# Grouped-query attention on one core: the P·V product of two groups as full-array matmuls of 256 columns in place of column-tiled ones

## The chip, the core and the metric

The kernel runs on one core of a Trainium2 chip. The metric is the device time of one execution in microseconds; the kernel before takes 348.19 us (median of three runs, 348.05 to 348.26). The profiled execution has a span of 346.9 us, and all times below that are counted from a start are counted from the start of that span.

The engines have short names in the profile: PE is the matrix engine TensorE (PEld its weight loads), DVE is VectorE, ACT is ScalarE, POOL is GpSimd, and SP is the engine whose queue issues nearly all DMA transfers here.

## The reference

```python
B, Hq, Hkv, Sq, Sk, D = 16, 32, 8, 16, 2048, 128      # all in bf16

def reference(q, k, v):
    rep = Hq // Hkv                                   # 4 query heads share one K and V
    k = jnp.repeat(k, rep, axis=1)
    v = jnp.repeat(v, rep, axis=1)
    scale = D ** -0.5
    scores = jnp.einsum("bhqd,bhkd->bhqk", q, k) * scale
    p = softmax(scores, axis=-1)
    return jnp.einsum("bhqk,bhkd->bhqd", p, v)
```

There are 16 x 8 = 128 groups. A group has 4 heads x 16 queries = 64 query rows, and one K and one V of 2048 x 128 elements, 512 KB each. So 128 MB of K and V are read for 4 MB of q and output.

## The kernel before, in words

**Pairs.** Two groups make a *pair* p (64 pairs, `NP`), so that their 2 x 64 query rows fill 128 partitions: group 0 of the pair (`gg = 0`) has partitions 0 to 63, group 1 has 64 to 127. Two neighbouring pairs, 2s and 2s+1, share their scores' layout and are worked on together.

**The steps of a pair**, by the names of the planner:

- `K` and `V` are loads of 1 MB each into one of 15 slots (`NSLOT`); the V of the last pair comes as two halves, `VH` 0 and 1. V of pair t-6 is issued after K of pair t (`LAG = 6`). L429 issues loads.
- `kx` (L354, DVE): K is transposed in 32 x 32 blocks from its slot into `KT`, two instructions for each K.
- `S` (L452, PE): 32 matmuls of 512 columns into `S_ps`, which fill half the keys' scores of both pairs 2s and 2s+1. `S_ps` is single: the next `S` waits until both exponentials of this one have read it.
- `ex` (L373, ACT): the exponential of 128 x 1024 scores into `P`, with the sum of each row; two for each pair.
- `pt` (L462, PE): 8 transposes of 128 x 128 into `PT_ps`, and `pe` (L399, ACT or DVE): the copy of these 1024 columns into `PT`. Two of each for a pair. There are three `PT` tiles, so the first copy of pair p waits for the product of pair p-3.
- `pv` (L468, PE): the product with V into `O_ps`. There is one `O_ps`, and `pv` of pair p waits until the scaling of pair p-1 has read it.
- `rs`, `rc` (L379, L384, DVE): the row sum and its reciprocal; `nm` (L388 on ACT, L390 on DVE): `O_ps` times the reciprocal, as bf16, into an output tile; `ST` (L426, L421) and `STA` (L381, the last half, issued by ACT): the stores.

**`pv` before** takes, for each of the 16 blocks of 128 keys, two matmuls: one for each group, with 64 weight columns (the group's columns of `PT`) and 128 moving columns (the group's V). The outputs lie one above the other, on partitions 0 to 63 and 64 to 127 of the same 128 columns of `O_ps`, so each matmul uses half of the columns of the PE array. One `nm` of 128 x 128 then covers both groups.

**The order of the work** is fixed before the kernel runs. `make_ops` (L47) writes down what each step depends on, and the order of the transfers. `build_schedule` (L135) is a greedy list planner: it always takes the step that can start first, by durations that are written into the table `_DUR` (L26), and puts it at the end of its engine's list; `nm` and `pe` may go to ACT or DVE, whichever would finish first. Each engine then runs its own list in order, and waits at a step for the semaphores of what that step depends on. V is taken by the planner to be ready 4 us after the end of its transfer (`_V_LATE`). So a number in `_DUR` does not change any instruction, but it can change the order in which an engine meets them, and which engine does a copy.

The kernel builds a second program (`general`) for inputs whose row sums leave a safe range; on these inputs it isn't run.

Of the kernel before, what the change touches and what calls it, by code (L numbers as in the profile page):

```python
# [14 lines left out]
NBO = 9  # L15
NKT = 2
NPT = 3
# [6 lines left out]


_DUR = {  # L26
    "qt": 0.55, "S": 1.1, "pt": 0.54, "pv": 1.08,
    ("dve", "kx"): 1.25, ("dve", "mx"): 1.25, ("dve", "nb"): 0.17, ("dve", "rs"): 0.17, ("dve", "rc"): 0.17,
    ("dve", "nm"): 0.36, ("dve", "pe"): 0.69, ("act", "pe"): 1.03, ("act", "qe"): 1.06, ("dve", "qe"): 1.25,
    ("act", "nm"): 0.42, ("act", "ex"): 1.27, ("act", "STA"): 0.4, ("pool", "qr"): 1.6, ("act", "qr"): 1.1, ("dve", "qr"): 1.1,  # L30
# [16 lines left out]
def make_ops(NP, pairs_per_chunk, general):  # L47

    deps = {}
    dma = []  # L50
    ch = lambda p: p // pairs_per_chunk
    n_ch = ch(NP - 1) + 1
    last_of = lambda c: min(NP, (c + 1) * pairs_per_chunk) - 1
    halves = (0, 1)

    def add(op, *d):
        deps[op] = [x for x in d if x is not None]

    opt = lambda ok, op: op if ok else None
    o_of = lambda p: p // 2 if p < NP - 1 else NP // 2  # L60
    v_of = lambda p: [("VH", x) for x in halves] if p == NP - 1 else [("V", p)]
    for c in range(n_ch):
        add(("Q", c), *[opt(c >= 2, ("qr", c - 2, x)) for x in range(4)])
        for x in range(4):
            prev = ("qe", c, x - 1) if x else opt(c >= 1, ("qe", c - 1, 3))
            add(("qr", c, x), ("Q", c), opt(c >= 1, ("qt", c - 1, x)))
            add(("qt", c, x), ("qr", c, x), prev)
            add(("qe", c, x), ("qt", c, x), opt(c >= 2, ("S", last_of(c - 2))))
    for p in range(NP):
        for load in [("K", p)] + v_of(p):  # L70
            add(load)
    for s in range(NP // 2):
        for gg in range(2):
            for h in halves:
                add(("kx", s, gg, h), ("K", 2 * s + gg), opt(s >= NKT, ("S", 2 * (s - NKT) + 1)))
    for u in range(NP):
        prev = [("mx" if general else "ex", 2 * ((u - 1) // 2) + pp, (u - 1) % 2) for pp in range(2)] if u else []
        add(("S", u), *[("kx", u // 2, gg, h) for gg in range(2) for h in halves],
            *[("qe", ch(2 * (u // 2)), x) for x in range(4)], *prev)
    for p in range(NP):  # L80
        for h in halves:
            u = 2 * (p // 2) + h
            if general:
                add(("mx", p, h), ("S", u), *[opt(p >= 2, ("ex", p - 2, x)) for x in halves])
            add(("ex", p, h), ("nb", p) if general else ("S", u), *[opt(p >= 2, ("pt", p - 2, x)) for x in halves])
        if general:
            add(("nb", p), ("mx", p, 0), ("mx", p, 1))
        for h in halves:
            add(("pt", p, h), ("ex", p, 0), ("ex", p, 1), opt(p >= 1, ("pe", p - 1, h)))
            add(("pe", p, h), ("pt", p, h), opt(p >= NPT, ("pv", p - NPT, 0)))  # L90
        for x, v in enumerate(v_of(p)):
            add(("pv", p, x), ("pe", p, 0), ("pe", p, 1), v, opt(p >= 1, ("nm", p - 1)))
        add(("rs", p), ("ex", p, 0), ("ex", p, 1))
        add(("rc", p), ("rs", p))
        add(("nm", p), ("pv", p, len(v_of(p)) - 1), ("rc", p), opt(o_of(p) >= NBO, ("ST", o_of(p) - NBO)))
        if p == NP - 2:
            add(("ST", p // 2), ("nm", p))
        elif p == NP - 1:
            add(("ST", NP // 2), ("nm", p))
            add(("STA", 0), ("nm", p))  # L100
        elif p % 2:
            add(("ST", p // 2), ("nm", p - 1), ("nm", p))
    qstep = {max(0, c * pairs_per_chunk - QLEAD): c for c in range(n_ch)}
    dma.append(("Q", 0))
    for t in range(NP + LAG):
        if t < NP:
            dma.append(("K", t))
        if qstep.get(t, 0):
            dma.append(("Q", qstep[t]))
        if t >= LAG:  # L110
            dma += v_of(t - LAG)
        if t - LAG - DSTORE in range(0, NP, 2):
            dma.append(("ST", (t - LAG - DSTORE) // 2))
    dma += [("ST", s) for s in range(NP // 2 + 1) if ("ST", s) not in dma]
    return deps, dma
# [95 lines left out]
def bass_standalone__gqa_softmax__sampling_kernel(  # L211
# [10 lines left out]
    NP = G // 2  # L222
# [121 lines left out]
    def elementwise(eng, me, prog, before_last=None):  # L344
        waits = prog.waiter(eng, me)
        for op in prog.progs[me]:
            kind, p = op[0], op[1]
            if before_last is not None and op == prog.progs[me][-1]:
                before_last()
            waits(op)  # L350
            mark_hint(eng, me, prog, op)
            if kind == "kx":
                _, _, gg, h = op
                ins = eng.transpose(KT[p % NKT][:, gg, :, h],  # L354
                                    prog.slot(("K", 2 * p + gg))[:, J * 64 * h:J * 64 * (h + 1)])
            elif kind == "qr":
                x = op[2]
                dst = Qr[:, x, :, :].rearrange("m i (a d) -> m i a d", a=4)
                src = bass.AP(Qn[p % 2], (x // 2) * 64 + x % 2, [[NI * 128, 128], [128, NI], [0, 4], [2, 32]])
                ins = eng.activation(dst, src, ACT.Copy) if me == "act" else eng.tensor_copy(dst, src)  # L360
            elif kind == "mx":
                h, part = op[2], slice(Sk // 2 * (p % 2), Sk // 2 * (p % 2 + 1))
                ins = eng.tensor_scalar(Sneg[p % 2][:, Sk // 2 * h:Sk // 2 * (h + 1)], S_ps[:, part], -scale, None,
                                        op0=ALU.mult, op1=ALU.min, accum_out=nhalf[:, p, h:h + 1])
            elif kind == "nb":
                ins = eng.tensor_tensor(nbias[:, p:p + 1], nhalf[:, p, 0:1], nhalf[:, p, 1:2], op=ALU.min)
            elif kind == "ex":
                h = op[2]
                if prog.general:
                    src = Sneg[p % 2][:, Sk // 2 * h:Sk // 2 * (h + 1)]  # L370
                else:
                    src = S_ps[:, Sk // 2 * (p % 2):Sk // 2 * (p % 2 + 1)]
                ins = eng.activation(  # L373
                    P[p % 2][:, :].rearrange("m (r a h j) -> m h a r j", h=2, a=2, j=32)[:, h],
                    src.rearrange("m (a r j) -> m a r j", a=2, j=32), ACT.Exp,
                    bias=nbias[:, p:p + 1] if prog.general else 0.0, scale=-1.0 if prog.general else scale,
                    accum_out=rhalf[:, p, h:h + 1])
            elif kind == "rs":
                ins = eng.tensor_tensor(rowsum[:, p:p + 1], rhalf[:, p, 0:1], rhalf[:, p, 1:2], op=ALU.add)  # L379
            elif kind == "STA":  # L380
                eng.dma_start(*out_rows(NP - 1, 1)).then_inc(*prog_sem(prog, op))  # L381
                continue
            elif kind == "rc":
                ins = eng.reciprocal(rrec[:, p:p + 1], rowsum[:, p:p + 1])  # L384
            elif kind == "nm":
                dst, src, r = o_tile(p), O_ps[:, 0:128], rrec[:, p:p + 1]
                if me == "act":
                    ins = eng.activation(dst, src, ACT.Copy, scale=r)  # L388
                else:
                    ins = eng.tensor_scalar(dst, src, r, None, op0=ALU.mult)  # L390
            else:
                if kind == "qe":
                    dst = QT[p % 2][:, op[2], :].rearrange("d (a i) -> d a i", i=NI)
                    src = QT_ps[:, 0:qch].rearrange("d (i a) -> d a i", i=NI)
                else:
                    h = op[2]
                    dst = PT[p % NPT][:, 8 * h:8 * (h + 1), :]
                    src = PT_ps[h][:, :].rearrange("k (t m) -> k t m", t=8)
                ins = eng.activation(dst, src, ACT.Copy) if me == "act" else eng.tensor_copy(dst, src)  # L399
            ins.then_inc(prog.sem_eng[me], 1)  # L400
# [30 lines left out]
    def matmuls(pe, prog):  # L431
        waits = prog.waiter(pe, "pe")
        for op in prog.progs["pe"]:
# [30 lines left out]
            else:  # L464
                rs = range(J) if p < NP - 1 else range(J // 2 * op[2], J // 2 * (op[2] + 1))
                for r in rs:
                    for gg in range(2):
                        ins = pe.matmul(  # L468
                            O_ps[64 * gg:64 * (gg + 1), 0:128],
                            PT[p % NPT][:, r, 64 * gg:64 * (gg + 1)],  # L470
                            prog.v_rows(p)[:, gg, r, :],
                            start=(r == 0), stop=(r == J - 1), skip_group_check=True,
                        )
            ins.then_inc(prog.sem_eng["pe"], 1)

    all_within = struct.unpack("<i", struct.pack("<f", 2.0 * 128 * NP))[0]
# [90 lines left out]
```

## Time and profile before

| | |
|---|---|
| time, median of three runs | 348.19 us |
| span of the profiled execution | 346.9 us |
| HBM read, written | 136.31 MB, 2.10 MB |
| DVE busy | 225.8 us |
| ACT busy | 226.6 us |
| a full stretch of the transfers, any of 40 us between 40 and 280 us | 412 to 414 GB/s |
| a `kx`, an `ex` | 1.23 us; 1.03 us and 0.20 us to read the row sums out |
| first `pv`, last `pv` begin | 29.7 us, 343.0 us |

The page shows busy time, and matmuls are pipelined: a matmul that is listed with 0.23 us may follow its neighbour by a small part of that. What a step of many matmuls costs is read from the timeline, where neighbouring instructions of one line are merged into one row with a start and a length. The chain of waits follows the work back from the last instruction, at each step to whatever released it. In a row of the chain or the timeline the first number is the start, the second the length, both in us.

### The profile page before, as it was taken

What the parts mean: (1) busy time and instruction counts of PE and PEld (TensorE: products, weight loads), DVE (VectorE), ACT (ScalarE), POOL (GpSimd) and SP (SyncE); (2) the same over time, 40 slices, a digit from 0 to 9 for tenths busy, and PEclk for the clock granted to TensorE, in tenths of its full rate; (3) what the DMA queues carried; (4) which work ended last, traced back from release to release, by engine and by line L of the source; (5) the groups of instructions that cost most, each with busy time, mean ns of one, the idle gap of its engine ahead of it and who ended that gap; (6) DMA issues with size and microseconds to landing.
All of it is one profiled execution on the core that took longest, in us unless ns stands there. A gap on an engine that the chain in (4) does not pass through costs nothing.

```text
span 346.9 us, 11937 instructions
## 1 busy us (share of the span) xinstructions
PE 238.6 (69%) x5378; PEld 172.7 (50%) x5378; DVE 225.8 (65%) x377; ACT 226.6 (65%) x369; POOL 29.0 (8%) x35
## 2 busy tenths in 40 slices
PE   1568868756686668766687665865857757576785
PEld 1345646534464446543465453643645545454564
DVE  4867996874775666746666655767559476576544
ACT  4496887665586575946759646787558746477551
POOL 1310031000400004000040000400004000000000
PEclk9998999999899898999989989999899989899899
DMA  7999999999999999999999999999999999999983
GB/s 309 426 412 415 411 413 412 412 415 414 411 418 415 412 412 414 415 413 414 413 412 417 414 415 414 414 413 415 413 413 414 412 417 416 414 412 412 392 336 108
DMA packets 37349, 139.21 MB, mean 401 GB/s; under 512 B 11440, under 2 KB 11440, under 8 KB 29104
## 3 DMA queue, kind: packets, MB, share of 16 engines
q1 hardware_dynamic: 37216, 138.41, 98.9%
q8 instruction: 43, 0.70, 0.8%
q14 instruction: 10, 0.08, 0.1%
q10 hardware_dynamic: 80, 0.02, 0.0%
HBM read 136.31 MB, written 2.10 MB: 399 GB/s over the span
## 4 chain that ended last, share of the span: by engine, by line
DMA 72%; DVE 11%; PE 9%; ACT 6%; issue 1%; SPq 0%; ACTq 0%
DMA slot<-in_k_dram 72%; DVE KT L354 9%; PE O_ps L468 3%; ACT P L373 2%; PE PT_ps L462 2%; PE S_ps L452 2%; PE QT_ps L440 1%; ACT QT L399 1%; DVE PT L399 1%; ACT PT L399 1%; DMA Qn<-in_q_dram 1%; DVE O L390 1%; ACT L360 0%; ACT Qr L360 0%; DVE rowsum L379 0%
## 5 line engine op out<-in xcount | busy, mean ns | idle before, releaser
L354 DVE STREAM_TRANSPOSE KT<-slot 128x1024 int32<-128x1024 int32 x128 | 154.5, 1231 | 101.3 <-DMA slot<-in_k_dram 92.8
L373 ACT ACTIVATE P<-S_ps 128x1024 bf16<-128x1024 f32 x128 | 130.5, 1025 | 87.5 <-PE PT_ps L462 49.6
L462 PE MATMUL PT_ps<-ident,P 128*128 128x128 bf16 x1024 | 74.4, 229 | 83.1 <-DVE PT L399 44.0
L462 PEld LDWEIGHTS PT_ps<-ident,P 128*128 128x128 bf16 x1024 | 62.3, 102 | 104.7 <-DVE PT L399 53.7
L452 PE MATMUL S_ps<-KT,QT 32*64 32x512 bf16 x2048 | 75.9, 401 | 11.0 <-ACT P L373 9.7
L468 PE MATMUL O_ps<-slot,PT 128*64 128x128 bf16 x2048 | 76.7, 233 | 1.3 <-DVE O L390 1.0
L468 PEld LDWEIGHTS O_ps<-slot,PT 128*64 128x64 bf16 x2048 | 65.9, 119 | 17.8 <-issue 14.2
L399 ACT ACTIVATE PT<-PT_ps 128x1024 bf16<-128x1024 bf16 x60 | 61.1, 1019 | 3.0 <-PE PT_ps L462 2.1
L360 POOL COPY Qr<-Qn 128x1024 bf16<-128x1024 bf16 x28 | 28.0, 1042 | 235.2 <-DMA Qn<-in_q_dram 235.2
L399 DVE COPY PT<-PT_ps 128x1024 bf16<-128x1024 bf16 x68 | 45.2, 668 | 1.8 <-PE PT_ps L462 1.8
L452 PEld LDWEIGHTS S_ps<-KT,QT 32*64 32x64 bf16 x2048 | 28.1, 106 | 32.3 <-ACT P L373 12.9
L440 PE MATMUL QT_ps<-ident,Qr 128*128 128x128 bf16 x256 | 22.1, 236 | 10.2 <-ACT Qr L360 6.1
L399 ACT ACTIVATE QT<-QT_ps 128x1024 bf16<-128x1024 bf16 x23 | 23.5, 1023 | 7.3 <-PE QT_ps L440 7.3
L373 ACT ACTIVATION_READ_ACCUMULATOR P<-S_ps 128x1 f32 x128 | 25.9, 202 | 0.0
L440 PEld LDWEIGHTS QT_ps<-ident,Qr 128*128 128x128 bf16 x256 | 16.7, 105 | 16.5 <-issue 8.3
L388 ACT ACTIVATE O<-O_ps,rrec 128x128 bf16<-128x128 f32 x27 | 9.9, 367 | 11.6 <-PE O_ps L468 11.6
L390 DVE TENSOR_SCALAR O<-O_ps,rrec 128x128 bf16<-128x128 f32 x37 | 12.0, 324 | 5.5 <-PE O_ps L468 5.4
L399 DVE COPY QT<-QT_ps 128x1024 bf16<-128x1024 bf16 x9 | 10.9, 1209 | 1.8 <-PE QT_ps L440 1.8
L379 DVE TENSOR_TENSOR rowsum<-rhalf 128x1 f32<-128x1 f32 x64 | 8.5, 152 | 4.4 <-ACT P L373 4.4
L384 DVE RECIPROCAL rrec<-rowsum 128x1 f32<-128x1 f32 x64 | 8.5, 153 | 0.5
L360 ACT ACT_TABLE_LOAD x1 | 1.3, 1283 | 3.6 <-DMA Qn<-in_q_dram 3.6
L360 DVE COPY Qr<-Qn 128x1024 bf16<-128x1024 bf16 x2 | 1.3, 690 | 3.5 <-DMA Qn<-in_q_dram 3.5
(13 smaller groups left out, 4.2 us busy)
## 6 DMA issues: line engine op xcount, KB each, us to landing
slot<-in_k_dram SPq DMA_DIRECT2D x64, 1024.0 KB, 17.6
slot<-in_v_dram SPq DMA_DIRECT2D x63, 1024.0 KB, 17.7
Qn<-in_q_dram SPq DMA_DIRECT2D x8, 256.0 KB, 15.3
out_dram<-O SPq DMA_DIRECT2D x62, 32.0 KB, 13.2
slot<-in_v_dram SPq DMA_DIRECT2D x2, 512.0 KB, 12.3
out_dram<-O SPq DMA_DIRECT2D x3, 16.0 KB, 1.8
out_dram<-O ACTq DMA_DIRECT2D x1, 16.0 KB, 2.0
```

Of the source, the lines that this page charges most:

```text
L354: ins = eng.transpose(KT[p % NKT][:, gg, :, h], prog.slot(("K", 2 * p + gg))[:, J * 64 * h:J * 64 * (h + 1)])
L360: ins = eng.activation(dst, src, ACT.Copy) if me == "act" else eng.tensor_copy(dst, src)
L373: ins = eng.activation(P[p % 2][:, :].rearrange("m (r a h j) -> m h a r j", h=2, a=2, j=32)[:, h], src.rearrange("m (a r j) -> m a r j", a ...
L379: ins = eng.tensor_tensor(rowsum[:, p:p + 1], rhalf[:, p, 0:1], rhalf[:, p, 1:2], op=ALU.add)
L384: ins = eng.reciprocal(rrec[:, p:p + 1], rowsum[:, p:p + 1])
L388: ins = eng.activation(dst, src, ACT.Copy, scale=r)
L390: ins = eng.tensor_scalar(dst, src, r, None, op0=ALU.mult)
L399: ins = eng.activation(dst, src, ACT.Copy) if me == "act" else eng.tensor_copy(dst, src)
L440: ins = pe.transpose(QT_ps[:, 128 * i:128 * (i + 1)], Qr[:, x, i, :], ident[:, :],)
L452: ins = pe.matmul(S_ps[64 * gg:64 * (gg + 1), 512 * a:512 * (a + 1)], QT[c % 2][32 * a:32 * (a + 1), x, row:row + 64], kt[:, :, x // 2, p ...
L462: ins = pe.transpose(PT_ps[h][:, 128 * t:128 * (t + 1)], P[p % 2][:, 128 * r:128 * (r + 1)], ident[:, :])
L468: ins = pe.matmul(O_ps[64 * gg:64 * (gg + 1), 0:128], PT[p % NPT][:, r, 64 * gg:64 * (gg + 1)], prog.v_rows(p)[:, gg, r, :], start=(r == 0 ...
```

## The change

One `pv` of a pair is made of 16 matmuls in place of 32. Each takes all 128 columns of a block of `PT` as weights (both groups' query rows) and the V of both groups, 2 x 128 columns, as the moving operand, so its output is 128 rows by 256 columns of `O_ps`. Of that, two blocks are wanted: rows 0 to 63 with columns 0 to 127 (group 0) and rows 64 to 127 with columns 128 to 255 (group 1). The other two blocks, one group's weights with the other's V, are computed and never read. The purpose is half the number of matmuls and weight loads, without column tiling.

Since the wanted blocks no longer lie in the same columns, `nm` is split into two steps of 64 rows by 128 columns, one for each group, and the planner may give them to different engines. What depended on `nm` of a pair now depends on both halves; of the last pair the store issued by SP needs only half 0, that issued by ACT only half 1. The last pair keeps two matmuls of 64 weight columns for each block, since its V comes in halves, but writes them to the two diagonal blocks. The planner's `pv` goes from 1.08 to 1.75 us.

```diff
 _DUR = {
-    "qt": 0.55, "S": 1.1, "pt": 0.54, "pv": 1.08,
+    "qt": 0.55, "S": 1.1, "pt": 0.54, "pv": 1.75,
...
         for x, v in enumerate(v_of(p)):
-            add(("pv", p, x), ("pe", p, 0), ("pe", p, 1), v, opt(p >= 1, ("nm", p - 1)))
+            add(("pv", p, x), ("pe", p, 0), ("pe", p, 1), v, *[opt(p >= 1, ("nm", p - 1, gg)) for gg in halves])
...
-        add(("nm", p), ("pv", p, len(v_of(p)) - 1), ("rc", p), opt(o_of(p) >= NBO, ("ST", o_of(p) - NBO)))
+        for gg in halves:
+            add(("nm", p, gg), ("pv", p, len(v_of(p)) - 1), ("rc", p), opt(o_of(p) >= NBO, ("ST", o_of(p) - NBO)))
+        mine, before = [("nm", p, gg) for gg in halves], [("nm", p - 1, gg) for gg in halves]
         if p == NP - 2:
-            add(("ST", p // 2), ("nm", p))
+            add(("ST", p // 2), *mine)
         elif p == NP - 1:
-            add(("ST", NP // 2), ("nm", p))
-            add(("STA", 0), ("nm", p))
+            add(("ST", NP // 2), mine[0])
+            add(("STA", 0), mine[1])
         elif p % 2:
-            add(("ST", p // 2), ("nm", p - 1), ("nm", p))
+            add(("ST", p // 2), *before, *mine)
...
             elif kind == "nm":
-                dst, src, r = o_tile(p), O_ps[:, 0:128], rrec[:, p:p + 1]
+                gg = op[2]
+                rows = slice(64 * gg, 64 * (gg + 1))
+                dst, src, r = o_tile(p)[rows, :], O_ps[rows, 128 * gg:128 * (gg + 1)], rrec[rows, p:p + 1]
...
                 for r in rs:
+                    edge = dict(start=(r == 0), stop=(r == J - 1), skip_group_check=True)
+                    if p < NP - 1:
+                        ins = pe.matmul(O_ps[:, 0:256].rearrange("m (g d) -> m g d", g=2), PT[p % NPT][:, r, :],
+                                        prog.v_rows(p)[:, :, r, :], **edge)
+                        continue
                     for gg in range(2):
-                        ins = pe.matmul(
-                            O_ps[64 * gg:64 * (gg + 1), 0:128],
-                            PT[p % NPT][:, r, 64 * gg:64 * (gg + 1)],
-                            prog.v_rows(p)[:, gg, r, :],
-                            start=(r == 0), stop=(r == J - 1), skip_group_check=True,
-                        )
+                        part = slice(64 * gg, 64 * (gg + 1))
+                        ins = pe.matmul(O_ps[part, 128 * gg:128 * (gg + 1)], PT[p % NPT][:, r, part],
+                                        prog.v_rows(p)[:, gg, r, :], **edge)
```

## The prediction

> **What bounds the kernel now.** I read the page first: busy time, the transfers over the span, the queues, the chain that ended last.
>
> ```profile
> PE 238.6 (69%) x5378; PEld 172.7 (50%) x5378; DVE 225.8 (65%) x377; ACT 226.6 (65%) x369; POOL 29.0 (8%) x35
> ...
> DMA  7999999999999999999999999999999999999983
> ...
> q1 hardware_dynamic: 37216, 138.41, 98.9%
> ...
> DMA 72%; DVE 11%; PE 9%; ACT 6%; issue 1%; SPq 0%; ACTq 0%
> ```
>
> No engine is busy more than 69%. The transfers fill every slice but the first and the last two. So over most of the span the kernel is a stream of loads, and other work costs time only if it stops the stream or comes after it. The waits, by who waited for whom, say what paces the engines, and the page's groups give the steps that the change touches:
>
> ```profile
> DVE KT L354 <- DMA slot<-in_k_dram: 92.8, 52, 3.7
> PE O_ps L468 <- DVE O L390: 1.0, 2, 0.5
> ```
>
> ```profile
> L468 PE MATMUL O_ps<-slot,PT 128*64 128x128 bf16 x2048 | 76.7, 233 | 1.3 <-DVE O L390 1.0
> L388 ACT ACTIVATE O<-O_ps,rrec 128x128 bf16<-128x128 f32 x27 | 9.9, 367 | 11.6 <-PE O_ps L468 11.6
> L390 DVE TENSOR_SCALAR O<-O_ps,rrec 128x128 bf16<-128x128 f32 x37 | 12.0, 324 | 5.5 <-PE O_ps L468 5.4
> ```
>
> DVE waits 52 times for a K that is just landing. A load lands 17.6 us after its issue (page, issues), about seven loads of 1 MB at 2.53 us, so a slot that comes free one or two us later doesn't empty the queue.
>
> Then the end. The last K is issued at 308.7 us and its first `kx` runs at 323.57; after that the stream brings V alone. The chain of waits over the last 29 us:
>
> ```profile
> 321.95 1.89 PE PT_ps L462 x16
> 323.84 1.64 PE O_ps L468 x32
> 325.48 0.02 issue
> 325.51 0.37 ACT O L388
> ...
> 327.85 1.07 PE PT_ps L462 x16
> 328.92 1.08 PE S_ps L452 x23
> 329.99 1.03 PE O_ps L468 x32
> 331.03 0.03 issue
> 331.05 0.36 DVE O L390
> 331.41 0.14 issue
> 331.55 1.08 PE O_ps L468 x32
> ...
> 339.61 1.01 PE O_ps L468 x32
> ...
> 341.49 1.10 PE O_ps L468 x32
> ```
>
> From 318.4 us on the chain holds no transfer: it runs through PE, ACT and DVE to the end, and five of the `pv` that the change lengthens lie on it (pairs 56, 57, 58, 61, 62; pair 63 keeps its form). Yet the stream's end isn't far off: the last half of V is issued at 330.8 us, lands at 343.3 by the trace's landing record, and the last `pv` runs from 343.02 to 344.10. So the end is bound twice, by the PE's chain and, less than 1 us behind, by the last V.
>
> **What the Trainium skill says.** *TensorE: Matmul & The Clock Gate*, "Back-to-back issue gap", gives a distance of N/2.4 + 2.5 ns for N moving columns at the full clock: 109 ns for 256. The trace agrees at the widths it has: in its timeline `pt`, with 128 columns, starts its transposes 56 ns apart, and `S`, eight tiles side by side of 512 columns, starts a new round about every 220 ns. *TensorEngine Tiling (Array Packing)*, "Theoretical Speedup", allows twice the speed for 64 weight columns; the trace agrees, as the two tiled matmuls of a block start 1 to 3 ns apart and blocks follow every 55 ns. "The HAM clock gate" on the first page has half the clock after idle windows of some 3.4 us. The trace shows eleven such stretches before the end, one from 321.7 to 325.1 us, in which `pv` took 1.64 to 1.9 us in place of 1.08.
>
> **The change part by part.**
>
> *Matmuls.* No row of before has 256 columns at full width. From below, half of the fastest 512-column round on the timeline (216 ns) is 108 ns; from above, two 128-column steps with a weight load each are 112 ns. I take 108. A `pv` was 16 x 55.5 = 0.89 us plus about 0.13 until the next step starts (1.02 on the timeline); it becomes 16 x 108 + 130 = 1.86 us, so **+0.84 us**. Column tiling already ran both groups side by side; the change computes two unwanted blocks and saves nothing. Half the weight loads go, but they lie beside the matmuls (`pt` loads 128 columns per transpose at 56 ns). Over 63 pairs that is +53 us of PE.
>
> *In the stream (pairs 0 to about 55).* A two-pair cycle is about 10.5 us. On the timeline from 201.96 to 213.44 PE idles 2.37 us (for DVE's copy of `PT`, itself behind the `kx` of a K just landed) and 1.28 us. Two longer `pv` take 1.68 of these 3.65. At the start, 34.66 to 42.42 us, where a backlog is worked off and K is not waited for, two pairs took 7.8 us; with 1.68 more that is 9.5, still under 10.5. So here **0**, hidden by the loads.
>
> *Split `nm`.* Both rows have 128 columns, and rows lie side by side, so each half costs as much as the whole: +0.31 us on DVE or +0.37 on ACT for each pair, some +21 us in all on engines that are 65% busy: 0 in the stream. `pv` of p+1 waits for both halves; side by side on the two engines 0, one behind the other +0.3. Behind the waiting `pv` on PE stand `pt` and `S`, and ACT's exponentials wait for these. At the end two such waits count (57 to 58, 62 to 63): 0 to 0.6, I take 0.2. The two stores of the last pair wait for one half each: 0.
>
> *The end.* I keep PE's order of before and walk along it. `pv` 56 delays its `nm`, ACT's copy, the exponential and `pt` at 327.85: +0.84 (less if busier PE avoids the half clock there). `pv` 57 and 58 stand one behind the other and then `pt`: +0.84 each. `pv` 59 lies beside an exponential that ends 0.26 us after it: +0.58; `pv` 60 the same with 0.30: +0.54. `pv` 61 and 62: +0.84 each. Sum 5.3. Against that: the last `pv` had waited some 0.2 us for the last V, the idle stretches (338.6 to 339.0, 341.2 to 341.5) can take some 0.5, and with 1.75 us in its table the planner can move a `pv` into another gap. From below: from 327.85 PE has six longer `pv` (6 x 1.86), the last (1.08), six halves of `pt` (3.0, with pair 60 4.0) and two `S` (2.2), 18.4 us, with no wait at all but 0.4 for the last `nm`: 346.7, which is 2.6 after 344.1. Between 2.6 and 5.3 I take +3.8, with `nm` **+4.0: 352.2 us**.
>
> **Rivals.**
>
> *A. Hidden to the end.* The planner moves the longer `pv` so that the end stays with the last V: 343.3 + 0.77 us as now. For it: in its table V comes 2.6 us apart, and PE idles in the twenty us before 344. Against it: the 18.4 us of PE work counted above don't fit into the 16.3 from 327.85 to 344.1. About 348.3 us, not slower.
>
> *B. PE becomes the bound throughout.* The backlog cycle would be 7.8 + 1.68 + 0.6 for split `nm` and 0.5 for its share of q's transposes = 10.6, above 10.5, and wherever the planner's order puts a `pv` ahead of an `S`, ACT waits. With 0.15 us too much per pair, 60 pairs lose 9, besides the end's 4: 361 us. Against it: the 3.65 us of idle per cycle. The backlog at the start would not go and the transfers would show gaps.
>
> *C. Faster.* Less idle on PE removes stretches of half clock, and another order packs the end better. But the last V lands at 343.3 whatever PE does, so at most some 0.7 us are to be had: 347.4.
>
> **How the numbers follow.** The forecast (slower by the end's `pv` alone) 0.68, A 0.14, B 0.12, C 0.06. Slower is the forecast and B: 0.80; same is A: 0.14; faster is C: 0.06. The bounds of the end give 350.8 to 353.7; a worse order, one more half clock or a `kx` phase shifted against the loads adds some us. To leave out no more than 2 in 10 the range takes in A and the nearer part of B: 348.0 to 358.0.
>
> **What would show it.** `pv` as 16 matmuls of about 1.9 us on the timeline; PE busy up by some 50 us to about 290; DMA still 9 in all the middle slices and DVE still waiting for K; the last V landing within 1 us of 343.3; the last `pv` beginning near 347 in place of 343.0, with no wait on V but a chain of PE steps without idle ahead of it. I am wrong if 256 columns follow each other faster than 100 ns, if the slices show gaps in the stream (B), or if PE waits for the last V as before (A).

## The result, and the profile after

The changed kernel takes 349.98 us (median of four executions, 349.48 to 350.76) against 348.18 us: a ratio of 1.0054 with a 95% interval of 1.0030 to 1.0078. Run once more beside the later experiments it gave 350.43 against 348.62 us, 1.0050 (1.0036 to 1.0064). So it is slower, as forecast, but by 1.8 us and not by 4.0. The question is where the other 2.2 us went.

The page of the kernel after: busy time, the granted clock of PE in forty slices, the transfers, the queues, and the chain by engine.

```profile
PE 273.3 (79%) x4370; PEld 198.9 (57%) x4370; DVE 260.0 (75%) x436; ACT 217.4 (63%) x374; POOL 28.9 (8%) x35
...
PEclk9999999999999999999999999999999999999999
DMA  7999999999999999999999999999999999999982
...
q1 hardware_dynamic: 37216, 138.41, 98.5%
q8 instruction: 35, 0.57, 0.7%
...
DMA 62%; PE 25%; ACT 6%; DVE 3%; issue 1%; SPq 1%; DVEq 0%
```

PE is 35 us busier and is still not full; its clock is at full speed from start to end. The transfers fill the same slices as before. PE's share of the chain has gone from 9% to 25%. Two rows of the page before, which the prediction does not show, turned out to matter:

```profile
PEclk9998999999899898999989989999899989899899
...
q8 instruction: 43, 0.70, 0.8%
```

Queue q8 brings instructions: 43 packets of 16 KB before, 35 after. PE has 2 x 5378 instructions before (matmuls and weight loads) and 2 x 4370 after, a difference of 2016. Eight packets fewer for 2016 instructions fewer are 65 bytes for each instruction.

The groups of the product and of the scaling, after:

```profile
L473 PE MATMUL O_ps<-slot,PT 128*128 128x256 bf16 x1008 | 120.8, 273 | 26.2 <-DMA slot<-in_v_dram 26.1
L392 ACT ACTIVATE O<-O_ps,rrec 64x128 bf16<-64x128 f32 x56 | 20.2, 362 | 55.7 <-PE O_ps L473 54.2
L394 DVE TENSOR_SCALAR O<-O_ps,rrec 64x128 bf16<-64x128 f32 x72 | 25.2, 350 | 38.4 <-PE O_ps L473 36.9
```

A half `nm` costs about as much as a whole one did, and there are twice as many. The waits after show another pace-maker:

```profile
PEld O_ps L473 <- DMA slot<-in_v_dram: 34.0, 40, 2.5
PE O_ps L473 <- DMA slot<-in_v_dram: 26.1, 38, 2.0
DVE KT L356 <- DMA slot<-in_k_dram: 10.2, 8, 1.6
```

Before, DVE waited 92.8 us for K, and a `pv` began 2.4 us (median of pairs 20 to 56) after its V had landed. Now PE waits for V, and `pv` begins at the landing: the planner, told that `pv` is longer, has put it earlier in PE's list. The chain of waits at the end of the kernel after:

```profile
307.32 17.27 DMA slot<-in_v_dram
324.60 0.05 issue
324.64 1.92 PE O_ps L473 x16
326.56 1.06 PE S_ps L456 x28
327.62 1.85 PE O_ps L473 x16
...
336.97 1.87 PE O_ps L473 x16
...
341.51 1.76 PE O_ps L473 x16
343.28 0.02 issue
343.30 0.37 ACT O L392
...
343.81 1.10 PE O_ps L478 x32
```

The V of pair 57 lands at 324.6 us, and from there PE works with two gaps of 0.7 and 0.5 us to the end of the last `pv` at 344.9. That is the tail of PE's work that was forecast. But the whole tail lies earlier: before, the V of pair 57 landed at 326.1 us, and the last V at 343.3; now they land at 324.6 and 341.1, by the trace's landing records. So:

- the loads come 1.5 us earlier at pair 57 (2.2 at the last V);
- from pair 57's V to the end of the last `pv` it takes 20.3 us in place of 18.0, which is +2.3 (counted from the landing of the last K it is +2.3 too);
- together the last `pv` ends at 344.9 in place of 344.1, +0.8, and the profiled execution's span grows by as much, from 346.9 to 347.7.

The profiled execution of before (348.72 us) lies 0.5 above its median, that of the change (349.49) 0.5 below: 0.8 + 0.5 + 0.5 is the 1.8 of the medians.

### The profile page after: what moved, and what is told of

It reads as the page before. It is cut to its first block, busy times and chain, and to the rows that moved or that the text cites. A ratio compares the mean times of both kernels' runs of the same rounds, so it can differ in the third digit from the quotient of the medians.

```text
span 347.7 us, 10053 instructions
## 1 busy us (share of the span) xinstructions
PE 273.3 (79%) x4370; PEld 198.9 (57%) x4370; DVE 260.0 (75%) x436; ACT 217.4 (63%) x374; POOL 28.9 (8%) x35
## 4 chain that ended last, share of the span: by engine, by line
DMA 62%; PE 25%; ACT 6%; DVE 3%; issue 1%; SPq 1%; DVEq 0%
DMA slot<-in_v_dram 54%; PE O_ps L473 12%; PE S_ps L456 9%; DMA slot<-in_k_dram 8%; ACT P L375 4%; PE PT_ps L466 3%; DVE KT L356 3%; ACT PT L403 1%; PE QT_ps L444 1%; ACT QT L403 1%; SPq L433 1%; PE O_ps L478 0%; DVE O L394 0%; DVE PT L403 0%; ACT O L392 0%
## 5 line engine op out<-in xcount | busy, mean ns | idle before, releaser
L473 PE MATMUL O_ps<-slot,PT 128*128 128x256 bf16 x1008 | 120.8, 273 | 26.2 <-DMA slot<-in_v_dram 26.1
L473 PEld LDWEIGHTS O_ps<-slot,PT 128*128 128x128 bf16 x1008 | 94.2, 98 | 45.5 <-DMA slot<-in_v_dram 34.0
L466 PE MATMUL PT_ps<-ident,P 128*128 128x128 bf16 x1024 | 71.9, 221 | 29.6 <-ACT P L375 28.9
L466 PEld LDWEIGHTS PT_ps<-ident,P 128*128 128x128 bf16 x1024 | 60.1, 98 | 55.1 <-ACT P L375 40.1
L456 PE MATMUL S_ps<-KT,QT 32*64 32x512 bf16 x2048 | 73.8, 392 | 5.8 <-ACT P L375 4.4
L403 DVE COPY PT<-PT_ps 128x1024 bf16<-128x1024 bf16 x89 | 59.3, 673 | 2.4 <-PE PT_ps L466 0.9
L392 ACT ACTIVATE O<-O_ps,rrec 64x128 bf16<-64x128 f32 x56 | 20.2, 362 | 55.7 <-PE O_ps L473 54.2
L394 DVE TENSOR_SCALAR O<-O_ps,rrec 64x128 bf16<-64x128 f32 x72 | 25.2, 350 | 38.4 <-PE O_ps L473 36.9
L403 ACT ACTIVATE PT<-PT_ps 128x1024 bf16<-128x1024 bf16 x39 | 39.6, 1016 | 3.0 <-PE PT_ps L466 2.9
L403 ACT ACTIVATE QT<-QT_ps 128x1024 bf16<-128x1024 bf16 x20 | 20.4, 1021 | 4.2 <-PE QT_ps L444 3.8
L403 DVE COPY QT<-QT_ps 128x1024 bf16<-128x1024 bf16 x12 | 14.4, 1200 | 0.2 <-PE QT_ps L444 0.2
```

The lines of the kernel that those rows point to most:

```text
L456: ins = pe.matmul(S_ps[64 * gg:64 * (gg + 1), 512 * a:512 * (a + 1)], QT[c % 2][32 * a:32 * (a + 1), x, row:row + 64], kt[:, :, x // 2, p ...
L466: ins = pe.transpose(PT_ps[h][:, 128 * t:128 * (t + 1)], P[p % 2][:, 128 * r:128 * (r + 1)], ident[:, :])
L473: ins = pe.matmul(O_ps[:, 0:256].rearrange("m (g d) -> m g d", g=2), PT[p % NPT][:, r, :], prog.v_rows(p)[:, :, r, :], **edge)
```

## The experiments

Two theories were set against each other. FETCH: PE's instructions come over the same DMA engines as K and V, so 2016 fewer instructions bring the loads home earlier. ORDER: the new order, in which `pv` starts at the landing of its V, moves the loads and the tail. All landings below are from the landing records of each run's trace.

| run | PE fetches (q8) | K 63 lands | V 57 lands | last V lands | last `pv` ends | ratio to before |
|---|---|---|---|---|---|---|
| before | 43 | 323.5 | 326.1 | 343.3 | 344.1 | 1 |
| change | 35 | 322.1 | 324.6 | 341.1 | 344.9 | 1.0054 (1.0030 to 1.0078) |
| order only | 43 | 323.6 | 326.0 | 342.8 | 343.7 | 1.0019 (1.0011 to 1.0027) |
| change, old duration | 35 | 322.1 | 324.6 | 341.5 | 345.5 | 1.0040 (1.0027 to 1.0053) |
| split only | 43 | 323.5 | 326.1 | 343.3 | 344.1 | 0.9992 (0.9984 to 1.0001) |
| tail tiled (8 pairs) | 36 | 322.0 | 324.6 | 341.4 | 343.6 | 0.9983 (0.9974 to 0.9993) |
| wide in the tail only | 43 | 323.5 | 326.0 | 341.7 | 347.5 | 1.0112 (1.0094 to 1.0129) |
| more PE fetches | 51 | 324.9 | 327.4 | 344.7 | 345.4 | 1.0039 (1.0025 to 1.0052) |
| tail tiled late (5 pairs) | 36 | 321.9 | 324.4 | 341.4 | 342.7 | 0.9978 (0.9964 to 0.9992) |
| GpSimd instructions | 43 | 326.7 | 329.1 | 344.8 | 346.0 | 1.0065 (1.0048 to 1.0083) |

**The order alone.**

```diff
-    "qt": 0.55, "S": 1.1, "pt": 0.54, "pv": 1.08,
+    "qt": 0.55, "S": 1.1, "pt": 0.54, "pv": 1.75,
```

> The kernel before with one number changed: the planner's duration of pv is 1.75 in place of 1.08 us. The instructions are those of before, their order on PE, DVE and ACT is a new one. FETCH theory (the loads land earlier after the change because PE has fewer instructions, so fewer 16 KB instruction fetches lie in the way on the same DMA rings): the same 5378 matmuls, so 43 fetches as before, last V at 343.3 us +-0.5 as before; pv may start right at the landing of its V, and the end stays within 0.2 us of before: 347.9 to 348.4 us. ORDER theory (the new order alone brings loads and the start of the tail forward): last V near 341.1 us, and with the short pv the end about 0.8 us after it: about 346.1 us.

Measured: 349.04 against 348.49 us. The chain of this run's last part:

```profile
308.79 17.26 DMA slot<-in_v_dram
326.05 0.04 issue
326.09 1.55 PE O_ps L468 x32
...
342.65 1.10 PE O_ps L468 x32
```

`pv` now starts at the landing of its V, but that landing is at 326.05 us as before: the order doesn't move the loads, and ORDER is out. It doesn't shorten the time either; with 0.5 us more than before it missed what FETCH expected (347.9 to 348.4) by some 0.6. In its trace the last `pv` ends 0.4 us earlier than before, but from there to the end of the span it takes 3.2 us in place of 2.8; why the median is 0.5 us longer stays open.

**The change, planned with the old duration.**

```diff
-    "qt": 0.55, "S": 1.1, "pt": 0.54, "pv": 1.75,
+    "qt": 0.55, "S": 1.1, "pt": 0.54, "pv": 1.08,
```

> The changed kernel with the planner's pv at 1.08 us as before, so planned as if nothing had become longer (nm split as in the change). FETCH theory: 35 fetches, last V near 341.1 us; PE's tail is that of the walk in the prediction, so the end comes 3 to 5 us after the last V: 349.5 to 352 us. ORDER theory: last V back at 343.3 us, pv some us after the landing of its V as before, the end as forecast: 352 to 353.5 us.

Measured: 349.94 us against 348.49. The chain:

```profile
328.75 1.87 PE O_ps L473 x16
...
344.38 1.10 PE O_ps L478 x32
```

Here `pv` again begins about 3.2 us (median) after its V, pair 57 at 328.75 us, and the tail after it has the same number of long `pv`. The loads land as in the change. The time is that of the change (the intervals of the two ratios overlap) and inside what FETCH expected: the new order is worth nothing measurable.

**The split of `nm` alone.** In the changed kernel, planned with 1.08, every pair takes the tiled form:

```diff
-                    if p < NP - 1:
+                    if p < 0:
                         ins = pe.matmul(O_ps[:, 0:256].rearrange("m (g d) -> m g d", g=2), PT[p % NPT][:, r, :],
```

> The matmuls of before (32 tiled ones for each pair, pv at 1.08 us in the plan), but each group's product written to its own 128 columns and nm split into two, as in the change. Costs of the split alone. FETCH theory: 43 fetches, last V at 343.3 us, the end as before or up to 0.6 us later: 348.2 to 348.8 us. Rival (the split, by freeing DVE or by another plan, is what moves the loads): last V near 341.1 us and about 346.5 us.

Measured: 348.38 against 348.49 us, no difference that can be told from the noise. The second `nm` of each pair is hidden.

**The wide form kept out of the tail.** The changed kernel, with the tiled form for the last eight pairs:

```diff
-                    if p < NP - 1:
+                    if p < NP - 8:
```

> The changed kernel, plan and all, but the last eight pairs use the 32 tiled matmuls (into the diagonal blocks) as only the last pair does in the change. The order of the steps is the same; PE's work after the last K is shorter by 7 x 0.84 us; 224 PE instructions more (about one fetch). If the end of the change is PE's tail: last V at 341.1 to 341.4 us, the end 0.8 to 1.2 us after it, 346.5 to 347.2 us, faster than both kernels. If the end hangs on something else (stores, nm, the order): 349 us or more, as the change.

Measured: 347.74 against 348.49 us, 0.17% faster than before, but 0.5 us above the top of what was expected. The reason stands in PE's timeline:

```profile
332.19 0.25 PE L478 MATMUL O_ps<-slot,PT 128*64 128x128 bf16 x2 [0.94 <-issue]
...
338.87 0.81 PE L466 MATMUL PT_ps<-ident,P 128*128 128x128 bf16 x11 [0.66 <-issue]
```

PE stops in the middle of a product and in the middle of its transposes, with no semaphore to wait for. By the trace's packet records q8 delivered 16 KB from 329.77 to 330.79 and from 336.41 to 337.40 us, so each time PE went on 1.4 to 1.5 us after a delivery ended. The two stops are 253 recorded PE instructions apart, about what one packet holds. So PE had run out of instructions: the tiled form uses 64 of them in 1.0 us, the wide one 32 in 1.85. The tail of the kernel before has one such stop as well: the 0.3 us ahead of pair 62's `pv` at 341.49, again 1.5 us after a delivery. The change's trace has none. What decides how late a packet comes stays open.

**Tiled only from pair 59.** With 128 instructions more than the change, in place of 224:

```diff
-                    if p < NP - 1:
+                    if p < NP - 5:
```

> The changed kernel, but pairs 59 to 62 use the 32 tiled matmuls (into the diagonal blocks), where the run with the last eight tiled had PE stop twice in the tail for an instruction fetch (0.9 and 0.7 us). Four pairs take 3.4 us from PE's tail with only 128 instructions more. If the tail is PE's work and those stops: one stop or none, the end 0.8 to 1.5 us after the last V (341.1 to 341.4), 346.6 to 347.4 us. If the tail is bound by the steps' dependencies: the same 347.7 us as with eight pairs tiled.

Measured: 347.70 against 348.62 us, 0.22% faster than before and the lowest median of all (the run with eight tiled pairs can't be told from it), though 0.3 us above the top of what was expected: in its trace the end of the span comes 3.2 us after the last `pv`, in place of 2.8. Its chain:

```profile
324.50 1.92 PE O_ps L473 x16
...
331.28 1.02 PE O_ps L478 x32
...
340.02 1.03 PE O_ps L478 x32
...
341.58 1.10 PE O_ps L478 x32
```

The stops are gone, and the last `pv` starts 0.2 us after the last V (341.4). It is released by the `nm` of the pair before it, so the end is bound twice again, as in the kernel before, and the loads are earlier. Against the change's second median of 350.43 us, taking four long `pv` out of the tail saves 2.7 us.

**The wide form in the tail alone.** The opposite: pairs 0 to 55 tiled, 56 to 62 wide, so PE has the number of fetches of before:

```diff
-                    if p < NP - 1:
+                    if NP - 8 <= p < NP - 1:
```

> The changed kernel, plan and all, but the wide matmuls only in pairs 56 to 62; pairs 0 to 55 use the 32 tiled ones (into the diagonal blocks). So PE has nearly the instructions of before (about 42 fetches) and the change's tail. FETCH theory: V of pair 57 lands at 325.8 to 326.1 us as before and not at 324.6 as in the change, the tail of 20.3 us from there on as in the change, so the end 1.3 us later than the change's: 350.5 to 351.5 us. Rival (the loads' earlier landing comes from the wide form's lower load on SBUF or from the order): V of pair 57 at 324.6, and 349.5 to 350 us as the change.

Measured: 352.86 us (351.94 to 353.55) against 348.62, +4.2 us: more than FETCH expected, and nearly what was forecast for the change. The V of pair 57 is back at 326.0 us. The chain of its slowest execution, the one with a trace:

```profile
320.86 3.18 PE O_ps L473 x16
...
346.41 1.10 PE O_ps L478 x32
```

The `pv` of pair 56 took 3.18 us in place of 1.92, since it fell into a stretch of half clock, as in the kernel before (the clock records of this trace have one from 321.3 to 324.7 us). The last `pv` ends at 347.5, which is 3.4 us later than before. The rest, up to 1.4 us, comes after it: 4.2 us to the end of the program in place of 2.8, because the store issued by SP took 1.2 us to issue and landed at 351.4; a fetch for PE ran from 347.8 to 348.7. Only the last V is earlier than before although PE has 43 fetches in all; the count of the fetches up to that moment, below, accounts for it.

**More fetches, on PE.** The kernel before, with this ahead of each `pv`:

```diff
+                for _ in range(19 if p < NP - 10 else 0):
+                    pe.matmul(O_ps[0:1, 511:512], ident[:, 0:1], ident[:, 0:1], start=True, stop=True,
+                              skip_group_check=True)
```

> The kernel before with 19 matmuls of one row and one column ahead of each pv of pairs 0 to 53, into a column of O_ps that nothing reads: 1026 more matmuls with their weight loads, 2052 instructions, 8 more fetches of 16 KB (51), and next to nothing after the last K. FETCH theory: eight fetches over the eight rings that carry them, one more each, so K of pair 63 lands 1.5 us later (325.0), V of pair 57 at 327.6, the last V near 344.9, the whole 1.3 to 1.8 us later: 349.6 to 350.3 us. Rival (PE's instructions have nothing to do with the loads): all landings and the time as before, 348.2 to 348.6 us.

Measured: 350.12 against 348.62 us, +1.5, inside what FETCH expected. The page's queue and, on DVE's timeline, the transposes of the last K, first of this run and then of before:

```profile
q8 instruction: 51, 0.84, 1.0%
```

```profile
324.87 2.37 DVE L354 STREAM_TRANSPOSE KT<-slot 128x1024 int32<-128x1024 int32 x2 [1.66 <-DMA slot<-in_k_dram]
```

```profile
323.57 2.37 DVE L354 STREAM_TRANSPOSE KT<-slot 128x1024 int32<-128x1024 int32 x2 [1.68 <-DMA slot<-in_k_dram]
```

Eight more fetches make the last K 1.3 us later, eight fewer (the change) make it 1.5 us earlier. This run also gives PE more work, but so does the change, and there the loads came earlier; so it is the fetches, not the work.

The records of the semaphore of a load show how. The Trainium skill, *DMA: Bandwidth & Descriptors*, "Why a DMA increments its semaphore by 16 and not by 1", says that a transfer runs on up to 16 engines which finish independently, and that each adds one when its part is there. For the last K the first part lands at 315.4 us in the kernel before and at 315.2 in the change and in this run, nearly the same; the last part lands at 323.5, 322.1 and 324.9. In the kernel before eight of the parts are 5.5 us and more ahead of the last, and eight within 2.1 us of it. So about half of the engines fall behind as the fetches add up, and a load is there only when the slowest has done its part.

The trace doesn't name the engine of a packet, but the count of the fetches shows how they are spread. If they go round eight engines, one after the other, then the slowest engine is worse off by one fetch with each new round of eight, and not with each fetch. So it is:

| K of pair | 19 | 23 | 35 | 39 | 63 |
|---|---|---|---|---|---|
| PE fetches done when it lands, before and change | 10, 8 | 12, 10 | 20, 16 | 23, 19 | 39, 31 |
| rounds of eight begun | 2, 1 | 2, 2 | 3, 2 | 3, 3 | 5, 4 |
| it lands earlier in the change by | 1.6 us | 0.3 | 1.7 | 0.4 | 1.5 |

Four fewer fetches are worth 1.7 us at pair 35 and 0.4 at pair 39. Over the K of pairs 14 to 63 in eleven traces (all but that of the next run), against the kernel before, a load lands 1.7 us earlier on average with one round fewer (197 loads), 0.2 earlier with as many (328) and 1.2 later with one more (25); the scatter about these three means is 0.15 us, while rounds of 4, 5, 6, 7, 9, 10, 12 or 16 leave 0.5 to 0.8 us, and a straight line in the number of fetches leaves 0.6. The last V fits too, in the same traces: it lands at 341.1 to 341.7 us in the runs with five rounds by then, the wide tail alone among them (40 fetches), at 342.8 to 343.3 with six and at 344.7 with seven.

**More instructions, on GpSimd.** The kernel before, with waits that are long fulfilled:

```diff
             ins.then_inc(prog.sem_eng[me], 1)
+            for _ in range(586 if me == "pool" and op[2] == 3 and not prog.general else 0):
+                eng.wait_ge(sem_id, 3)
```

(Two such waits become one instruction: 2051 more.)

> The kernel before with 2051 more instructions on GpSimd, which is busy 8% of the span: waits on a semaphore that has long been set, 293 after each of the last seven rounds of Qr copies, no data moved. About as many instructions as the run with more PE instructions has. If any fetched instruction takes time from the slowest DMA rings: K of pair 63 at 325.0 us, the last V near 344.9, 349.6 to 350.2 us. If only PE's fetches lie in the way (its rings are the slowest, other engines' instructions come by others, or in smaller pieces): K of pair 63 at 323.5, the last V at 343.3, the time as before within 0.3 us.

Measured: 350.92 against 348.47 us, +2.45: even more than FETCH expected. The page's queues and the last K:

```profile
q8 instruction: 43, 0.70, 0.8%
q14 instruction: 27, 0.22, 0.2%
```

```profile
326.68 2.38 DVE L354 STREAM_TRANSPOSE KT<-slot 128x1024 int32<-128x1024 int32 x2 [1.60 <-DMA slot<-in_k_dram]
```

PE's fetches are as before; another queue has 17 packets of 8 KB more within the span. The last K is 3.1 us later, and this time one part of the load is 3.5 us behind all the others. No data is moved by these instructions, and each round of them ends, after some 26 us, well before the next Qr copies, so that no copy waits for them: their fetching does it, on GpSimd as on PE. The part that comes last falls behind the next to last as the packets add up, from 0.1 us at the K of pair 3 to 4.0 at pair 53, where in the kernel before the two are never more than 1.7 us apart. That fits GpSimd's packets all lying on a single DMA engine, which would be why they cost more than PE's; no run tests it.

**The change again, for its spread.**

> The changed kernel as it is, for more executions beside the other runs on one chip: 349.5 to 350.7 us by all theories.

> The changed kernel once more, for its trace: its executions lie between 349.3 and 350.8 us, and both traces so far are of the fastest. If a slower one is caught: with the loads' landings as in the fast ones (V of pair 57 at 324.5 us) the difference is in PE's tail or after the last pv; with later landings it is in the stream.

> As the look before: the changed kernel once more, to catch a slower execution. Landings as in the fast traces (V of pair 57 at 324.5 us) put the difference into the tail or the end of the program, later ones into the stream.

Measured: 350.43 us (349.33 to 350.63), 349.83 and 350.08 us. In all four traces of the change the V of pair 57 lands at 324.4 to 324.6 us and the last `pv` ends at 344.7 to 344.9. What differs comes after it: 2.8 us to the end of the span in the two fastest, 3.2 and 3.5 us in the two others. There the next fetch for PE begins at 344.8 and 345.5 us, beside the last stores, and in the last one ACT's store needs 2.8 us to land in place of 1.9; in the two fastest that fetch begins only after 347.1. So up to 0.7 us of the change's spread may be one instruction fetch that falls among the last stores or doesn't. This is read from four traces and not tested; the run with the new order alone has 3.2 us with no PE fetch between 343.1 and 346.5, so there is another cause as well.

## Why the prediction was right or wrong

- **`pv` +0.84 us.** Right. Consecutive wide matmuls start 109 ns apart, and a `pv` takes 1.85 us until the next step in the chain, where it took 1.02.
- **PE +53 us.** Too much: +34.7. In part this is because PE's clock has no half-speed stretch left, so its other steps became shorter too (`pt` from 74.4 to 71.9 us in all, `S` from 75.9 to 73.8).
- **In the stream: 0.** This is the step that failed. It was right that the loads hide PE's work: no slice of the transfers shows a gap, and PE's longer `pv` delays no load. But the loads were taken as given ("the last V lands at 343.3 whatever PE does"), and they weren't: the change takes 2016 instructions, eight fetches of 16 KB, out of the stream's way. With eight more fetches the kernel before lost 1.5 us; the change gains as much at pair 57's V. The term is **-1.5 us in place of 0**. The page's row for q8 had shown the fetches.
- **Split `nm` 0.2 us.** Nothing measurable (ratio 0.9992, interval to 1.0001).
- **The end +3.8 us.** The mechanism is right: a chain of PE steps almost without idle time. The size is not: it measured **+2.3 us**. With the fetches of before, the wide form in the tail alone makes the last `pv` end 3.4 us later than before, near the forecast. In the change the walk's first term (pair 56, +0.84) fell away with the half clock: its `pv` took 1.92 us against 3.18 in the run with the wide tail alone. The forecast had named this ("less if busier PE avoids the half clock there") and put it at nothing. From 3.4, less 1.5 for the fetches and 1.3 for the half clock, 0.6 is left for the 0.8 by which the last `pv` ends later in the change's trace. That the clock made pair 56 shorter is read from the clock records, which have no half-clock stretch within the change's span; no run varies the clock alone.
- **The planner moves a `pv`.** It did, for nearly every pair from 9 to 57, and it was worth nothing measurable: 349.94 us with the old order, 349.98 and 350.43 with the new.
- **Rivals.** A fell: the end did not stay with the last V, which now lands 3.8 us before the last `pv` ends. B fell: no gaps in the stream. C named the half clock and a better end, and allowed them 0.7 us at most because the landing of the last V was taken as fixed; the half clock did go, and with the tail kept tiled the kernel beats the one before (0.9978).
- **Two readings.** The last `pv` of the kernel before had not waited for the last V: its matmuls run without a break from 343.02 us, and the half of V that lands at 343.33 is first used at 343.49. And the section "Back-to-back issue gap" of *TensorE: Matmul & The Clock Gate* gives N/2.4 + 2.5 ns for an isolated matmul; for a stream of matmuls with weight loads it gives 81 ns at 128 columns. This kernel's streams have 56 ns at 128 columns and 109 ns at 256, so the prediction was right to go by the trace.

## What to carry to other kernels

Where a kernel is a stream of loads, the instructions are part of the stream: read the page's instruction queues, and count what an edit adds or removes in instructions, on PE and on an engine that is nearly idle as well. Here the cost came in steps: eight PE fetches fewer were worth a step of about 1.5 us, four fewer a whole step or nearly nothing, depending on the load. A form that is slower on its engine but has fewer instructions can pay in the part that the loads hide and cost in the part after the last load; so choose the form for each part by itself. When an end is bound twice within a microsecond, check what moves the second bound before it is called fixed.

## What the runs showed of the hardware that had not been expected

- 2016 PE instructions fewer or 2052 more move the last K by 1.5 us earlier or 1.3 us later. The landings follow rounds of eight fetches: a step of some 1.4 us with each round, although a fetch takes about 1.05 us of one engine's time.
- 2051 instructions on GpSimd, in 8 KB packets, cost 2.45 us of the kernel's time.
- PE can run dry: with the last eight pairs tiled it stopped for 0.9 and 0.7 us in the tail, and went on 1.4 to 1.5 us after a fetch had been delivered. In the trace of the run with more fetches it stopped so nine times within a group of matmuls (0.2 to 1.7 us), each time 1.4 to 1.5 us after a delivery, and the stops lie 254 or 255 recorded instructions apart, or a multiple of that.
